# Memory attention and two MLPs on one core: PSUM tiles of two banks, table loads ahead of use, a root by Newton steps, and another order at the start

## The chip, the core and the metric

The kernel runs on one core of one Trainium2 chip. Five engines work side by side on that core, each with its own instruction queue: PE (TensorE, the matrix products), DVE (VectorE), ACT (ScalarE), POOL (GpSimd) and SP (SyncE, which here only starts transfers). Products land in PSUM, which has eight banks of 512 fp32 numbers for each of 128 partitions; everything else lies in SBUF. The metric is the device time of one execution in microseconds (us), the median of several runs.

## The reference, cut to what matters

There are 4 batches, 8 heads, 576 positions, a head width of 64 and 32 memory slots. The attention runs through the memory slots, and two MLPs follow on all 2304 positions of width 512.

```python
def _attn_ref(q, k, v, phi):
    a = np.exp(phi - np.max(phi, axis=2, keepdims=True))
    a = a / (np.sum(a, axis=2, keepdims=True) + 1e-09)      # over positions
    k_m = np.einsum('bhsm,bhsd->bhmd', a, k)
    v_m = np.einsum('bhsm,bhsd->bhmd', a, v)
    scores = 1.0 / np.sqrt(q.shape[-1]) * np.matmul(q, k_m.transpose(0, 1, 3, 2))
    scores = np.exp(scores - np.max(scores, axis=-1, keepdims=True))
    attn = scores / (np.sum(scores, axis=-1, keepdims=True) + 1e-09)   # over 32 slots
    return np.matmul(attn, v_m)

def _moe_ref(x, w_in, w_out):            # 512 -> 2048 -> 512
    h = x @ w_in
    return (h * (1.0 / (1.0 + np.exp(-1.702 * h)))) @ w_out

def _moe2_ref(x, w_gate, w_val, w_out, rms_g):   # 512 -> 1536 -> 512
    rms = np.sqrt(np.mean(x * x, axis=-1, keepdims=True) + 1e-06)
    xn = x / rms * rms_g
    g = xn @ w_gate
    return (g * (1.0 / (1.0 + np.exp(-g))) * (xn @ w_val)) @ w_out
```

## The kernel before

**Numbers in two parts.** Most products are made with operands split into a high part (fp32r) and a low part, the remainder: three products, high by high, low by high and high by low, stand for one of full precision. So each value that PE uses again is first copied by ACT (high part) and then subtracted by DVE or POOL (low part): `split()` at L858, `sub_lo()` at L744. Names that end in h and l, or an index 0 and 1, are such parts.

**Stages.** Batches are taken in pairs (pr 0 and 1), heads in two groups of four (g 0 and 1).

- Attention, for each batch and group: `att_k1t` or `att_k1` takes the maximum of phi over positions within a partition, `att_k2` and `att_k3` carry it over partitions (tiles pk2, pk3) and make the exponentials, `att_k4` multiplies them with k and v and makes their sums as products with a column of ones (tile pk4, `ones_f`), then the reciprocals rv, and `att_k5` brings km and vm into place (kz, vz, pk5). `att_q1` transposes q (pq1), `att_q3` makes the scores (pq3), their maximum and exponential, `att_q3s` the sums and the division, `att_q4` transposes the softmax result and splits it into attnT (pq4). Batch 0 is tiled by 64 positions: there the softmax result lies in two halves of the partitions, ACT copies it into a wider tile with zeros (`wide_e`, memset by DVE), and `att_q4` multiplies each of nine blocks with twin, a matrix of two stacked identities. Other batches are tiled by 96.
- First MLP, eight groups of 256 of the 2048 columns: `vm_part` multiplies the first weights into vm (tile pvm), so that `a_g1` (tile pg, lhsT vm, rhs attnT) gives the MLP's first layer at once; the first pg product from attnT and vm is what is called the first main product. The activation, a copy and a subtraction follow (gf, gr). `a_g2` multiplies gr with the second weights and DVE adds into x.
- Norm: `norm_1` squares and sums, `norm_2` sums over partitions by a product (pnr), ACT takes the root and DVE the reciprocal, `norm_3` and `norm_4` scale x.
- Second MLP, six groups of 256 columns as two units f each: `s_g3` makes gate and value by seven products of halves of the operands instead of eight, each product on 320 and 256 columns in a PSUM tile each (ps_A, ps_S), ACT copies out of PSUM, DVE adds and multiplies; `s_g4` multiplies with the output weights, 512 columns in a tile, and DVE adds into oacc; `put()` stores the rows.
- Weights come in blocks of 512 KB; ACT, DVE and POOL convert them (`w_conv`: pad, then a_inh and a_inl, or cv) and write them to caches in DRAM for the second pair.

**What sets the order.** All instructions of these steps go through one recorder and come from one line, L644, so tiles tell them apart. The steps are recorded in program order; class Plan groups them into units, gives each a due time (`dues()`: PE's main line is laid end to end, all else is due some time ahead of the unit that needs it), and simulates the five engines with a table of costs. `order()` takes at each step the unit that can start earliest, by due time among those that are near. Two tables change it: HASTE moves the due time of a named step earlier, OTHER moves single instructions of a named step between DVE and POOL. Where PE would idle ahead of a new PSUM tile, `fill()` puts dummy products of ones_r by ones_r (512 or 128 columns) into that tile. PSUM tiles are handed out in this order too:

```python
psp = pool("ps", 8, bass.MemoryType.PSUM, spare=2, ahead=4)
def psum(name):
    return psp.tile([P, 512], F32, tag="ps", name=name)
```

`can()` leaves spare slots for PE's main line, and ahead is how many tiles of the main line may be open before the due times press for the release of the oldest. An activation whose function lies in another table than the last one's makes the compiler put a table load right ahead of it on ACT.

## Time and profile before

| | before |
|---|---|
| median of 3 runs, us | 848.54 (847.63 to 848.97) |
| the profiled execution: its time, us | 843.96 |
| the profiled execution: its span, us | 842.2 |
| PE busy, us (share of the span) | 827.5 (98%) |
| DVE busy | 655.1 (78%) |
| ACT busy | 494.0 (59%) |
| POOL busy | 296.4 (35%) |

The span runs from the first to the last instruction of one profiled execution; the time of that execution lies 1.8 us above it. Busy time is summed over an engine's instructions, and PE's includes the dummy products and products that run at a lower clock. A row of the timeline holds consecutive instructions of one form with their start, their time together, and the idle time ahead of them with what ended it. An fp32 product (both operands fp32) shows as two records in a row of PE, a product of fp32r operands as one.

### The profile page before, as it was taken

What the parts mean: (1) busy time and instruction counts of PE and PEld (TensorE: products, weight loads), DVE (VectorE), ACT (ScalarE), POOL (GpSimd) and SP (SyncE); (2) the same over time, 40 slices, a digit from 0 to 9 for tenths busy, and PEclk for the clock granted to TensorE, in tenths of its full rate; (3) what the DMA queues carried; (4) which work ended last, traced back from release to release, by engine and by line L of the source; (5) the groups of instructions that cost most, each with busy time, mean ns of one, the idle gap of its engine ahead of it and who ended that gap; (6) DMA issues with size and microseconds to landing.
All of it is one profiled execution on the core that took longest, in us unless ns stands there. A gap on an engine that the chain in (4) does not pass through costs nothing.

```text
span 842.2 us, 16000 instructions
## 1 busy us (share of the span) xinstructions
PE 827.5 (98%) x5789; PEld 787.4 (93%) x5789; DVE 655.1 (78%) x1363; ACT 494.0 (59%) x1222; POOL 296.4 (35%) x295
## 2 busy tenths in 40 slices
PE   7999999999999999999999999999999999999997
PEld 6899999999999999999999999999999999999996
DVE  7978999999998998989989888767775435545555
ACT  4687878687778757666577755435552443323321
POOL 4444555666344556455846510120450000000000
PEclk9989999999999999999999999999999999999999
DMA  9964757856848776665676478463455543514314
GB/s 340 271 214 144 236 204 206 275 192 188 278 170 279 253 237 222 211 217 190 219 256 230 165 276 287 163 238 131 157 163 168 184 147 104 200 55 171 126 50 113
DMA packets 76767, 166.99 MB, mean 198 GB/s; under 512 B 7312, under 2 KB 29328, under 8 KB 76688
## 3 DMA queue, kind: packets, MB, share of 16 engines
q1 hardware_dynamic: 76688, 165.97, 59.5%
q8 instruction: 46, 0.75, 0.4%
q14 instruction: 33, 0.27, 0.1%
HBM read 106.69 MB, written 59.24 MB: 197 GB/s over the span
## 4 chain that ended last, share of the span: by engine, by line
PE 78%; DVE 10%; DMA 4%; issue 3%; ACT 3%; POOL 2%; SPq 0%; POOLq 0%; ACTq 0%; DVEq 0%
PE pg L644 42%; PE ps_A L644 21%; PE ps_S L644 9%; DVE pad L644 3%; PE pvm L644 2%; DVE x L644 2%; PE pq L644 2%; PE pk L644 1%; DMA stage<-in_q_dram 1%; DVE kmisc L644 1%; DVE stage L644 1%; DVE cv L644 1%; DMA stage<-in_v_dram 1%; DMA raw_c_gate<-in_moe_w_gate_dram 1%; DMA raw_a_out<-in_moe_w_out_dram 1%
## 5 line engine op out<-in xcount | busy, mean ns | idle before, releaser
L644 PE MATMUL pg<-gr,a_outh 128*128 128x384 f32 (+1 forms) x736 | 195.2, 334 | 0.8 <-POOL gr L644 0.6
L644 PEld LDWEIGHTS pg<-gr,a_outh 128*128 128x128 f32 x736 | 132.7, 188 | 2.4 <-POOL gr L644 2.0
L644 PE MATMUL pg<-gr,a_outl 128*128 128x384 f32 (+1 forms) x368 | 121.9, 331 | 0.0
L644 POOL TENSOR_TENSOR gr<-gf,gr 128x288 fp32r<-128x288 f32 (+2 forms) x118 | 83.8, 727 | 101.1 <-ACT gr L644 52.4
L644 PE MATMUL pg<-s_o,pp 128*128 128x512 f32 x432 | 114.0, 391 | 0.0
L644 ACT COPY c<-ps_A 128x320 f32<-128x320 f32 (+1 forms) x144 | 57.2, 399 | 93.7 <-PE ps_A L644 91.8
L644 DVE TENSOR_TENSOR x<-x,pg 128x384 f32<-128x384 f32 (+1 forms) x172 | 88.9, 535 | 11.0 <-PE pg L644 9.7
L644 DVE TENSOR_TENSOR oacc<-oacc,pg 128x512 f32<-128x512 f32 x90 | 61.7, 686 | 45.7 <-PE pg L644 44.9
L644 PEld LDWEIGHTS pg<-s_o,pp 128*128 128x128 f32 x432 | 79.0, 188 | 14.6
L644 PE MATMUL ps_A<-tba,s_A 128*128 128x320 f32 (+1 forms) x576 | 88.5, 296 | 0.0
L644 PEld LDWEIGHTS ps_A<-tba,s_A 128*128 128x128 f32 x576 | 81.9, 190 | 1.6
L644 DVE TENSOR_TENSOR c<-c,ps_S 128x320 f32<-128x320 f32 (+1 forms) x96 | 43.2, 452 | 37.6 <-PE ps_S L644 29.3
L644 PEld LDWEIGHTS pg<-gr,a_outl 128*128 128x128 f32 x368 | 69.1, 188 | 0.0
L644 ACT ACTIVATE gf<-pg 128x288 f32<-128x288 f32 x128 | 50.5, 412 | 31.1 <-PE pg L644 27.4
L644 ACT CAST gr<-gf 128x288 fp32r<-128x288 f32 (+2 forms) x184 | 59.2, 363 | 6.9 <-PE pg L644 4.3
L644 PE MATMUL pg<-s_o,tbd 128*128 128x512 f32 x216 | 61.1, 392 | 0.0
L644 DVE TENSOR_TENSOR c<-c 128x256 f32<-128x256 f32 (+1 forms) x86 | 39.3, 466 | 18.3 <-ACT c L644 16.6
L644 POOL TENSOR_SCALAR pad<-pad 128x512 f32<-128x512 f32 x20 | 41.2, 2062 | 19.9 <-ACT pad L644 19.7
L644 POOL TENSOR_SCALAR cv<-cv 128x512 f32<-128x512 f32 x20 | 44.1, 2210 | 8.1 <-ACT cv L644 6.5
L644 PE MATMUL ps_A<-tbc,s_S 128*128 128x256 f32 (+1 forms) x288 | 46.0, 297 | 0.0
L644 PE MATMUL ps_A<-tbd,s_A 128*128 128x320 f32 (+1 forms) x288 | 45.7, 297 | 0.1
L644 PE MATMUL ps_S<-tbb,s_S 128*128 128x256 f32 (+1 forms) x288 | 45.8, 296 | 0.0
(234 smaller groups left out, 1881.5 us busy)
## 6 DMA issues: line engine op xcount, KB each, us to landing
cache_s<-s_S SPq DMA_DIRECT2D x24, 512.0 KB, 3.7
s_S<-cache_s SPq DMA_DIRECT2D x24, 512.0 KB, 3.5
cache_b<-cv SPq DMA_DIRECT2D x36, 256.0 KB, 4.5
raw_a_in<-in_moe_w_in_dram SPq DMA_DIRECT2D x16, 512.0 KB, 5.3
raw_a_out<-in_moe_w_out_dram SPq DMA_DIRECT2D x16, 512.0 KB, 5.4
raw_c_gate<-in_moe_w_gate_dram SPq DMA_DIRECT2D x12, 512.0 KB, 4.7
raw_c_val<-in_moe_w_val_dram SPq DMA_DIRECT2D x12, 512.0 KB, 4.3
raw_c_o<-in_moe_w_out_dram SPq DMA_DIRECT2D x12, 512.0 KB, 4.4
```

The costliest lines, as they stand in the source:

```text
L644: getattr(self.real[op.eng], op.name)(*op.args, **op.kw)
```

## The change

- **PSUM.** Four tiles of two banks (`both()`) take the place of eight of one (`psum()` gives the first half of such a tile); spare goes from 2 to 1 and ahead from 4 to 2. Steps that used two tiles side by side now use one: `a_g1` both halves of its 256 columns, `a_g2` two blocks of 128 outputs, `s_g3` two times 288 columns instead of 320 and 256, `s_g4` two blocks of 128 positions, except in its last group. The instruction of ACT or DVE that empties a tile takes both banks at once (`pair()`), 576, 768 or 1024 columns. The SBUF pools follow: cv is 5 times 576 columns for 6 times 512, gp 3 tiles of double size for 6.
- **Order records.** A tile is tracked by bank (q, m), so a copy out of one bank doesn't order itself against writes of the other.
- **Table loads.** `issue()` puts a one-column activation (into the tile pre, from a constant) right ahead of each activation whose function lies in another table than the last one's. The load goes with it, and neither waits for the data of the activation behind them. The root leaves ACT, so its table is not loaded any more.
- **Norm.** `norm_2` makes the reciprocal root on DVE: a first value from the bits of x, then three Newton steps, on three columns.
- **Batch 0.** `att_k3s` adds up the nine blocks of exponentials to three column blocks (512, then 256 columns), and `att_k4` has three products with the column of ones for nine. `att_q4` transposes by 32-column pieces against the identity, 72 products for 18 with twin; the copies into the wide tile and twin are gone. The memset of the stage tile goes from DVE to ACT.
- **Other batches.** `att_k1` (a strided reduction) is replaced by `att_k1t` (additions of the maximum kind), the sum in `att_k3s` likewise. `att_q1`, `att_q3`, `att_q3s` and `att_q4` treat both halves in one instruction.
- **Planner.** HASTE and OTHER are new, and some costs are changed. The tail of the last group is recorded as nine single tiles.

Counts by the recorded order: DVE 1365 instructions before and 1026 after, ACT 1224 and 776, POOL 297 and 217. The columns and number of PE's main products stay.

```diff
-SETS = {AF.Exp: 1, AF.Gelu_apprx_sigmoid: 2, AF.Silu: 3, AF.Sqrt: 4}
+SETS = {AF.Exp: 1, AF.Gelu_apprx_sigmoid: 2, AF.Silu: 3}
...
-        "a_g1 0 0 1": 19.4,
...
+        "w_load a 0 0 out 1": 615.4,
...
-                    q, m, write = 15, 1, True
+                    c = x.offset % 1024
+                    far = c + sum(st * (n - 1) for st, n in list(x.ap)[1:])
+                    q, m, write = 15, (1 if c < 512 else 0) | (2 if far >= 512 else 0), True
...
+            table = None
             for _, _, op in self.order():
+                func = op.kw.get("func") if op.eng == "ACT" else None
+                if func in SETS and SETS[func] != table:
+                    table = SETS[func]
+                    self.real["ACT"].activation(out=self.pre, in_=self.one, func=func)
                 getattr(self.real[op.eng], op.name)(*op.args, **op.kw)
...
-    cvp = pool("cv", 6, spare=3)
+    cvp = pool("cv", 5, spare=2)
...
-    gpp = pool("gp", 6)
+    gpp = pool("gp", 3)
...
-    psp = pool("ps", 8, bass.MemoryType.PSUM, spare=2, ahead=4)
+    psp = pool("ps", 4, bass.MemoryType.PSUM, spare=1, ahead=2)
...
+    def both(name):
+        return psp.tile([P, 1024], F32, tag="ps", name=name)
+
     def psum(name):
-        return psp.tile([P, 512], F32, tag="ps", name=name)
+        return both(name)[:, :512]
+    def pair(x, n):
+        return x.rearrange("p (q n) -> p q n", q=2)[:, :, :n]
...
     def att_k3s(u, eng):
         km = kmisc[u]
+        if u[0] < N9:
+            y = kmisc[u, "sums"] = cv("y")[:, :512]
+            e = stage[u][:, 3456:4480]
+            eng.tensor_tensor(out=y, in0=e[:, :512], in1=e[:, 512:], op=ALU.add)
+            eng.tensor_tensor(out=y[:, :256], in0=y[:, :256], in1=y[:, 256:], op=ALU.add)
+            return
...
     def att_q4(u, par):
-            for i, c in enumerate(some(par)):
-                PE.matmul(
-                    ps[:, R9 * i : R9 * i + R9], lhsT=qm[:, 3456 + P * c : 3456 + P * c + P], rhs=twin,
-                    start=True, stop=True,
-                )
+            for i in range(len(some(par))):
+                for o in range(4):
+                    t, rows = o // 2, slice(R9 * (o % 2), R9 * (o % 2) + R9)
+                    PE.matmul(
+                        ps[32 * o : 32 * o + 32, R9 * i : R9 * i + R9], lhsT=sm[rows, i, t],
+                        rhs=ident[rows, rows], start=True, stop=True,
+                    )
...
     def norm_2(pr, t):
-        A.activation(
-            out=r[:, 0, 0:3], in_=ps[:, 0:TB:P], func=AF.Sqrt, bias=epst, scale=1.0 / DM
+        V.tensor_scalar(
+            out=x, in0=ps[:, 0:TB:P], scalar1=1.0 / DM, scalar2=EPS, op0=ALU.mult, op1=ALU.add
         )
-        V.reciprocal(out=r[:, 1, 0:3], in_=r[:, 0, 0:3])
+        V.tensor_scalar(
+            out=zi, in0=x.bitcast(U32), scalar1=1, scalar2=None, op0=ALU.logical_shift_right
+        )
+        V.tensor_scalar(
+            out=yi, in0=zi, scalar1=-1.0, scalar2=float(0x5F3759DF), op0=ALU.mult, op1=ALU.add
+        )
+        for i in range(3):
+            V.tensor_tensor(out=z, in0=y, in1=y, op=ALU.mult)
+            V.scalar_tensor_tensor(out=z, in0=z, scalar=-0.5, in1=x, op0=ALU.mult, op1=ALU.mult)
+            V.scalar_tensor_tensor(out=y, in0=z, scalar=1.5, in1=y, op0=ALU.add, op1=ALU.mult)
...
-            for q in range(2):
-                product(pr, q, "S3", "T3", f, part[q]["a"])
-                x = part[q]["v"]
-                A.copy(out=x, in_=part[q]["a"])
-                V.tensor_tensor(out=x, in0=x, in1=part[q]["b"], op=ALU.add)
-                A.activation(out=x, in_=x, func=AF.Silu)
+            product(pr, "S3", "T3", f, part["a"])
+            x = full(part["v"])
+            A.copy(out=x, in_=pair(part["a"], HALF))
+            V.tensor_tensor(out=x, in0=x, in1=pair(part["b"], HALF), op=ALU.add)
+            A.activation(out=x, in_=x, func=AF.Silu)
...
-    for step in late + waiting:
-        line(*step)
-    plan.ones = ones_r
+    for kk in range(PT // P):
+        line(s_g4, 1, NB - 1, kk, False)
+    plan.ones, plan.one, plan.pre = ones_r, ones_f, pre
```

**Three places in the order.** The first is SP's queue from the program's start: kmisc is phi, stage holds k, v and q of a batch and group, raw_a are blocks of the first MLP's weights. Before:

```order
L644 DMA kmisc0_0_114<-in_phi_dram 128x288 x2
L644 DMA raw_a_0_0_in_0_118<-in_moe_w_in_dram 128x2x512
L644 DMA raw_a_0_0_in_1_119<-in_moe_w_in_dram 128x2x512
L644 DMA stage0_0_115<-in_v_dram 128x2x576
L644 DMA stage0_0_115<-in_k_dram 128x2x576
L644 DMA kmisc0_1_116<-in_phi_dram 128x288
L644 DMA raw_a_0_0_out_0_156<-in_moe_w_out_dram 128x1024
L644 DMA kmisc0_1_116<-in_phi_dram 128x288
L644 DMA stage0_0_115<-in_q_dram 128x2x576
```

After:

```order
L593 DMA raw_a_0_0_in_0_117<-in_moe_w_in_dram 128x2x512
L593 DMA raw_a_0_0_in_1_118<-in_moe_w_in_dram 128x2x512
L593 DMA raw_a_0_0_out_0_155<-in_moe_w_out_dram 128x1024
L593 DMA kmisc0_0_113<-in_phi_dram 128x288 x2
L593 DMA kmisc0_1_115<-in_phi_dram 128x288 x2
L593 DMA stage0_0_114<-in_k_dram 128x2x576
L593 DMA stage0_0_114<-in_v_dram 128x2x576
L593 DMA stage0_1_116<-in_k_dram 128x2x576
L593 DMA stage0_1_116<-in_v_dram 128x2x576
```

Three weight blocks now stand ahead of phi, and k and v of both groups come ahead of both q.

The second is DVE's queue at the same place, behind the constants: pad is a weight block under conversion, y and kmisc carry the maximum of phi. Before:

```order
L1602 TENSOR_TENSOR twin_93<-ident_90 128x64
L644 MEMSET stage0_1_117 128x1152
L644 TENSOR_TENSOR y_123<-kmisc0_0_114 128x192
L644 TENSOR_TENSOR y_123<-y_123,kmisc0_0_114 128x192
L644 TENSOR_TENSOR kmisc0_0_114<-y_123 128x64
L644 TENSOR_TENSOR kmisc0_0_114<-kmisc0_0_114,y_123 128x64
L644 TENSOR_REDUCE kmisc0_0_114<-pk2_124 64x2
L644 TENSOR_TENSOR kmisc0_0_114<-kmisc0_0_114,pk3_125 128x576
L644 TENSOR_SCALAR pad_120<-pad_120 128x512 x3
```

After:

```order
L593 TENSOR_SCALAR pad_119<-pad_119 128x512 x2
L593 SCALAR_TENSOR_TENSOR pad_119<-raw_a_0_0_in_0_117,pad_119 128x512
L593 TENSOR_SCALAR pad_119<-pad_119 128x512
L593 SCALAR_TENSOR_TENSOR pad_119<-raw_a_0_0_in_0_117,pad_119 128x512
L593 TENSOR_SCALAR pad_119<-pad_119 128x512
L593 SCALAR_TENSOR_TENSOR pad_119<-raw_a_0_0_in_1_118,pad_119 128x512
L593 TENSOR_TENSOR y_122<-kmisc0_0_113 128x192
L593 SCALAR_TENSOR_TENSOR pad_119<-raw_a_0_0_in_1_118,pad_119 128x512
L593 TENSOR_TENSOR y_122<-y_122,kmisc0_0_113 128x192
L593 TENSOR_TENSOR y_140<-kmisc0_1_115 128x192
L593 TENSOR_TENSOR kmisc0_0_113<-y_122 128x64
```

The memset and twin are gone, weight steps have moved ahead of the first maximum, and the second group's maximum stands among the first group's.

The third is PE in the second MLP of the second pair, near the end: ps_A11, ps_A12 and ps_S1 are tiles of `s_g3`, pg4 of `s_g4`. Before:

```order
L644 MATMUL ps_A11_1681<-tba1_1419,s1_11_A11_1662 128x320 x6
L644 MATMUL pg4_1674<-s1_8_o2_1600,pp_1626 128x512 x3
L644 MATMUL pg4_1674<-s1_9_o2_1622,tbd1_1422 128x512 x3
L644 MATMUL ps_A11_1682<-tba1_1419,s1_11_A11_1662 128x256 x6
L644 MATMUL ps_A12_1683<-tba1_1419,s1_11_A11_1662 128x320 x6
L644 MATMUL ps_A11_1681<-tbb1_1420,s1_11_S1_1663 128x320 x6
L644 MATMUL ps_A11_1682<-tbb1_1420,s1_11_S1_1663 128x256 x6
L644 MATMUL ps_A12_1684<-tba1_1419,s1_11_A11_1662 128x256 x6
L644 MATMUL ps_S1_1687<-tbb1_1420,s1_11_S1_1663 128x320 x6
L644 MATMUL ps_S1_1688<-tbb1_1420,s1_11_S1_1663 128x256 x6
L644 MATMUL ps_A11_1681<-tbc1_1421,s1_11_S3_1664 128x320 x6
L644 MATMUL ps_A11_1682<-tbc1_1421,s1_11_S3_1664 128x256 x6
```

After:

```order
L593 MATMUL ps_A11_1191<-tbb1_1019,s1_11_S1_1179 128x288 x12
L593 MATMUL ps_A12_1192<-tba1_1018,s1_11_A11_1178 128x288 x12
L593 MATMUL ps_A11_1191<-tbc1_1020,s1_11_S3_1180 128x288 x12
L593 MATMUL pg4_1195<-s1_8_o2_1138,pp_1155 128x512 x3
L593 MATMUL pg4_1195<-s1_9_o2_1153,tbd1_1021 128x512 x3
L593 MATMUL pg4_1195<-s1_8_o2_1138,pp_1155 128x512 x3
L593 MATMUL pg4_1195<-s1_9_o2_1153,tbd1_1021 128x512 x3
L593 MATMUL ps_A11_1191<-tbd1_1021,s1_10_A22_1165 128x288 x12
L593 MATMUL ps_S1_1194<-tbb1_1019,s1_11_S1_1179 128x288 x12
```

The products of 320 and 256 columns into two tiles have become 12 of 288 into one, and three products or more still stand between the first product on a tile and the next that is added onto it (ps_A11 and ps_A12 here).

## Rows read from the trace of the kernel before

**Rows 1.** The page, part 1: busy time, share of span, instructions.

```profile
PE 827.5 (98%) x5789; PEld 787.4 (93%) x5789; DVE 655.1 (78%) x1363; ACT 494.0 (59%) x1222; POOL 296.4 (35%) x295
```

**Rows 2.** The chain of waits, its end: start us, us, what.

```profile
823.47 1.60 PE ps_S L644 x12
825.07 12.28 PE pg L644 x54
```

**Rows 3.** Table by windows: stretch, us, busy us (count) by engine, PEclk, DMA, GB/s.

```profile
0.00:20.00 20.00, 15.46 (x130) 12.66 (x131) 15.27 (x40) 9.41 (x19) 9.26 (x14) 1.00 0.94 336
...
40.00:60.00 20.00, 19.03 (x177) 18.41 (x178) 15.24 (x39) 15.34 (x44) 9.84 (x11) 0.83 0.67 212
...
180.00:200.00 20.00, 19.86 (x137) 18.90 (x137) 19.93 (x43) 17.11 (x45) 16.49 (x16) 1.00 0.72 245
```

**Rows 4.** Timeline of PE: start us, us, op, out<-in, shapes, xcount [idle before, releaser].

```profile
1.25 3.62 PE L644 MATMUL pk<-ones_r 128*128 128x512 f32 x10 [1.25 <-DVE ones_r L1604]
...
10.36 2.19 PE L644 MATMUL pk<-stage 128*64 128x128 f32 x36 [1.83 <-DMA stage<-in_k_dram]
12.48 2.17 PE L644 MATMUL pk<-ones_f,stage 128*128 128x1 f32 x18
...
25.41 1.55 PE L644 MATMUL pq<-twin,stage 128*128 128x64 f32 x12
...
36.42 1.52 PE L644 MATMUL pk<-stage,kmisc 96*32 96x128 f32 x48
...
38.12 0.94 PE L644 MATMUL pq<-ident,stage 96*128 96x96 f32 x9
...
45.12 2.13 PE L644 MATMUL pq<-kmT,stage 128*96 128x64 f32 x12
...
47.01 0.83 PE L644 MATMUL pg<-attnT,vm_0h 128*128 128x288 f32 x2
...
50.98 1.15 PE L644 MATMUL pq<-kmT,stage 128*96 128x64 f32 x12
```

**Rows 5.** Timeline of DVE, 0 to 60 us.

```profile
3.98 0.30 DVE L644 TENSOR_TENSOR y<-kmisc 128x192 f32<-128x192 f32 x1
...
12.35 1.41 DVE L644 TENSOR_TENSOR y<-kmisc 128x192 f32<-128x192 f32 x1 [0.21 <-DMA kmisc<-in_phi_dram]
...
15.02 0.15 DVE L644 TENSOR_SCALAR rv<-pk 128x1 f32<-128x1 f32 x1
```

**Rows 6.** Timeline of ACT, 0 to 60 us.

```profile
7.92 1.36 ACT L644 ACTIVATE stage<-kmisc 64x576 f32<-64x576 f32 x2
```

**Rows 7.** Timeline of POOL, 0 to 60 us.

```profile
12.27 2.61 POOL L644 TENSOR_TENSOR a_inl<-pad,a_inh 128x512 fp32r<-128x512 f32 x2 [3.33 <-ACT a_inh L644]
14.85 2.02 POOL L644 TENSOR_SCALAR pad<-pad 128x512 f32<-128x512 f32 x1
...
40.70 1.46 POOL L644 TENSOR_SCALAR rv<-maskeo,rv 128x3 f32<-128x3 f32 x1 [1.09 <-DVE rv L644]
```

**Rows 8.** Groups by form: names, shapes, xcount | busy us, mean ns | idle before, releasers.

```profile
L644 DVE TENSOR_TENSOR x<-x,pg 128x384 f32<-128x384 f32 x156 | 81.8, 544 | 9.6 <-PE pg L644 8.4
...
L644 DVE TENSOR_TENSOR oacc<-oacc,pg 128x512 f32<-128x512 f32 x90 | 61.7, 686 | 45.7 <-PE pg L644 44.9
...
L644 ACT ACT_TABLE_LOAD x28 | 35.9, 1283 | 2.7 <-PE pg L644 1.5 <-PEq L1807 0.7
...
L644 ACT COPY c<-ps_A 128x320 f32<-128x320 f32 x72 | 30.7, 426 | 52.5 <-PE ps_A L644 51.7
```

**Rows 9.** Tile x, 100:240: DVE's additions (ns min/median/max); below, idle before (us, times).

```profile
L644 DVE TENSOR_TENSOR x<-x,pg x65: 441/542/555, 100.5 to 239.2; 128x384 f32<-128x384 f32 x62, 128x288 f32<-128x288 f32 x3
...
  PE pg L644: 1.6, 2
```

**Rows 10.** Waits of PE, 60 to 240 us: total us, times, longest.

```profile
PE pvm L644 <- DVE a_inl L644: 0.8, 1, 0.8
...
PE pg L644 <- POOL gr L644: 0.2, 1, 0.2
```

More of the change, by code (lines that the diff above doesn't have):

```diff
@@ L1238, in att_q3s @@
         eng.tensor_tensor(out=sm, in0=sm, in1=over_m(y), op=ALU.mult)
-        if u[0] < N9:
-            c = some(hp)
-            for r in range(2):
-                rows = slice(R9 * r, R9 * r + R9)
-                A.copy(out=wide_e(u)[rows, c[0] : c[-1] + 1, :, r], in_=sm[rows])
     def att_q4(u, par):
@@ new lines, in places @@
+    def places(pr, f):
+        if f % 3 == 0:
+            x = tb[pr, "tbd"][:, 1].rearrange("p y e n -> p y (e n)")
+            return [(0, x)]
+        if f % 3 == 1:
+            x, y = [gpp.tile([P, 2, 2, TB], F32R, tag="gp", name="pp") for i in range(2)]
+            part["rest"] = y[:, 1]
+            return [(0, x.rearrange("p a y n -> p (a y n)").rearrange("p (y n) -> p y n", y=2)), (2 * TB, y[:, 0])]
+        x = gpp.tile([P, 2, 2, TB], F32R, tag="gp", name="pp")
+        return [(0, part["rest"]), (TB, x.rearrange("p a y n -> p (a y n)").rearrange("p (y n) -> p y n", y=2))]
@@ L1521, in s_g3, with full @@
     def s_g3(pr, f, k):
+        def full(x):
+            return x.rearrange("p (q n) -> p q n", q=2)
         if k == 0:
-            c = [cvp.tile([P, 512], F32, tag="cv", name="c")[:, :320] for i in range(4)]
-            part[0] = dict(zip(("p", "u", "v", "s"), c))
-            c = [vlp.tile([P, 512], F32, tag="vl" + x, name="c") for x in "hl"]
-            part[1] = dict(zip(("p", "u", "v", "s"), [x[:, o : o + 256] for x in c for o in (0, 256)]))
-            for q in range(2):
-                part[q]["a"] = product(pr, q, "A11", "B11", f)
-                A.copy(out=part[q]["p"], in_=part[q]["a"])
@@ L1601 @@
     make_identity(nc, ident)
-    nc.vector.tensor_tensor(out=twin, in0=ident[:, :R9], in1=ident[:, R9:], op=ALU.add)
     nc.vector.memset(ones_f, 1.0)
@@ L1778 @@
                 late += waiting
-                waiting[:] = [(s_g4, int(key[0] == "s"), f // 2, kk) for kk in range(9)]
+                waiting[:] = [(s_g4, int(key[0] == "s"), f // 2, kk) for kk in range(5)]
         elif width(*key[1:]) == HALF:
```

531 lines of the change are left out of this document (293 added, 238 removed), and 119 rows, old and new, of the table OTHER.

## Prediction

> **What bounds the kernel now.** The page comes first: PE is busy 98% of the span, the next engine, DVE, 78% [rows 1]. Busy is not full rate, so I then looked at PE's steps in the chain of waits. Near the end twelve products (320 or 256 columns) take 1.60 us, and the last 54, of 512 columns, take 12.28 us, 0.227 us each, back to back [rows 2]. The change leaves the number and the columns of the main products as they are (six of 320 and six of 256 columns become twelve of 288, the same 3456). So the main work has a fixed price, and only time in which PE lacks work can be won. The table by windows shows where that is [rows 3]: PE is busy 15.5 us of the first 20, and 19.9 from 180 to 200 us, where DVE has no room left (19.9 of 20). [...] The same 12 records of a product take 2.13 us at 45.12 and 1.15 us at 50.98 [rows 4].
>
> The start is worse than its idle time says, because the planner puts dummy products into gaps (from ones_r, into the next tile). They count as busy: ten records and 3.62 us at 1.25 [rows 4], 33 wide ones by the order ahead of the first main product, which starts at 47.01 us (pg from attnT). I followed the chain that leads there: k and v of batch 0 land (PE waits to 10.36), products with k, their sums against a column of ones, the softmax on DVE and POOL, the transposition by twin, the splitting into two parts [rows 4 to 7].
>
> **The change part by part.** *Sums by fewer products.* Per head group, nine products with a one-column operand become three. Nine take 2.17 us at 12.48 (18 records, two a product) [rows 4], 0.24 each; 12 fewer: -2.9 us of PE work, all ahead of the first main product. In their place stand two additions per group, over 512 and 256 columns: about 0.69 and 0.40 us on DVE by the rows by form [rows 8], 1.3 us for 512 on POOL [rows 7], where the order puts one of each width. *Transposition.* 18 products with twin (six, twelve records, take 1.55 us, 0.26 each [rows 4]) become 72 with 32-column weights. Nearest is the row of 24 products with such weights and twice the columns (1.52 us for 48 records, 0.063 a product [rows 4]): that is the upper end, 4.6 us against 4.7, half of it the lower. I take 0.05, 3.6 us: -1.1 us. Eight ACT copies of the softmax result leave the same chain. These savings count inside the start below, not beside it.
>
> *The order of the start.* Three weight blocks now load ahead of phi, k and v, and eight DVE steps on weights stand ahead of the first group's first maximum. I walked the new order with durations from before. At 336 GB/s [rows 3] the three blocks of 512 KB take some 5 us, k and v of the first group are in at 12 us, of the second at 15, both q at 19. DVE's weight steps, at 0.4 to 0.7 us by their 512 columns [rows 8], put the last maximum near 11 us; until then 30 dummy products of 0.23 to 0.36 us fill PE. Both groups now go side by side: exponentials end at 15 and 17 us (9.3 for the first group before [rows 6]), both k products with their sums at 22 us, one group's reciprocals wait behind a POOL step of 1.46 us [rows 7], the scores are there at 24 and 28 us, the softmax steps of both groups (some 20 DVE steps of 0.2 to 0.55 us, with one POOL step on weights of 2.0 us among POOL's multiplications [rows 7]) end at 36, and the first main product starts at **37 us**, the value I take. The ends: 33 if no POOL step stands in the way; 42 by the first rival.
>
> From 47.0 to 37.0 is -10.0 us, but not all of it is won. Work of batch 1 that stood ahead of 47.0 now follows: 24 products with their sum 1.7 us, twelve transpositions of q 1.3, scores 1.1 [rows 4], six products with wide 0.8 (half of twelve [rows 2]), small ones an estimated 0.6: +5.5. Net **-4.5 us** (-8.5 to +0.5). Right after 37 us PE needs wide, which ACT and DVE split only behind attnT, and then vm of the second group, four more splits with some 3 us of other DVE steps ahead; the order has four dummy products there. I put PE's waits to 60 us at **+1.5 us** net (0 to +3). [...]
>
> *Wider steps on the other engines.* DVE's addition from PSUM takes 544 ns over 384 columns and 686 over 512 [rows 8]: 1.1 ns a column and 0.12 us fixed. The order has 1026 DVE instructions for 1365, although the Newton steps add 69 at 0.15 us or a little more (the step on one column takes 0.15 [rows 5]), 10 to 14 us. Some 400 removed at 0.12 us are 48 us; with the memsets and the strided sums gone too, DVE falls by about 40 of 655 us, by about 12 of 135 from 100 to 240 us. PE's named waits from 60 to 240 us are five, of 0.8 to 0.2 us [rows 10], 1.8 us together, and I estimate as much again in late starts inside rows that count as busy. Their cause, a full DVE queue and what waits for it, is mostly removed: **-3.5 us** (0 to -5). ACT and POOL do the same columns in half the instructions and are not full [rows 1]. Seven table loads of 1283 ns leave ACT, 21 one-column activations come. Their cover is ACT's idle time (41%); without it 9 us would count. The load stood right ahead of the instruction that needs it, and ACT's idle time before all 28 that PE ended is 1.5 us [rows 8]: loading early is worth that at most, and I count it at nothing.
>
> *Two-bank tiles.* Where a product is added onto a tile that was just copied, the order has other products between, at all 96 such places: at least six of 512 columns, 1.36 us, against a copy of 576 columns of at most 0.77 us (426 ns for 320, in proportion [rows 8]). Past the start a slot is nearly always written again 1.6 us or more after its last product (before: 2.7 or more, by the same steps). **+0.5 us** (0 to +17, third rival). The end stays: single tiles, then an addition and the store.
>
> **Sum.** -4.5 + 1.5 - 3.5 + 0.5 = **-6.0 us**: span 842.2 to 836.2. The profiled execution took 843.96 us, 4.6 less than the median of the runs, 848.54; I carry the difference over: **842.5 us**, by itself 837 to 846.5.
>
> **Rivals.** *The start is no earlier.* DVE's addition over 192 columns takes 0.30 us at 3.98 and 1.41 us at 12.35 [rows 5], while POOL runs two subtractions of SBUF operands (12.27 to 14.88) [rows 7]. The change puts two additions, a subtraction and a weight step on POOL between 15 and 21 us, beside DVE's additions and subtractions of the same chain. If four of these are held up by 1.1 us each, the first main product starts at 41 to 42: net +0.5, +2 after it, -2.5 in the middle: 848.5 us. For it: these two rows. Against: few of DVE's steps at 15 to 21 us are on the chain itself. [...] *Everything goes as ordered.* Start at 33, no new waits, all waits of the middle gone: -8.5 - 5 = -13.5: 835 us. Against it: before, the order held 33 wide dummy products, at most 12 us at 0.36, while PE lacked work for some 21 of the first 47 us. *Slower: half as many PSUM slots.* From 100 to 240 us DVE waited for PE ahead of only 2 of 65 additions into x [rows 9]: it is late, and sets when a slot is free. With four slots PE has half the lead. If DVE stays full, each of the 86 double additions holds PE for the smallest named wait of before, 0.2 us: +17 us, and the 3.5 are not won: 863 us, 854 if half of them wait. It decides by DVE's busy time in those windows; I expect 18 of 20, it needs over 19.3.
>
> **How the numbers follow.** Forecast 0.57, as ordered 0.16, start no earlier 0.12, slower 0.15. About 0.2% (1.7 us) is what a measurement here can tell from no change, so 846.8 to 850.2 is "same". Faster: 0.57 + 0.16, less a little at the edge, 0.72; same 0.13; slower 0.15. The range leaves out the third rival and what of the second lies below 832: 832 to 850.
>
> **What would show it.** Right: the first pg product from attnT at 35 to 39 us, the one-column products at 0.7 us per group; DVE near 615 us busy and 18 of 20 from 100 to 240. Wrong: a first main product after 41 us; PE waiting for DVE x or ACT c after 60 us; steps of twelve products over 1.60 us; the 72 products over 0.06 us each.

## The result

The changed kernel takes **839.38 us** (median of four runs, 839.12 to 841.09), the kernel before 848.75 us beside it: a ratio of 0.9894, 95% interval 0.9875 to 0.9912. That is 9.4 us less where 6.0 were forecast, and inside the range of 832 to 850. The profiled execution took 841.09 us, its span 839.3. Its span is thus only 2.9 us below the 842.2 from which the sum started; the sum put it at 836.2.

The page of the changed kernel, part 1, and its table by windows (columns as in [rows 1, 3]):

```profile
PE 823.3 (98%) x5890; PEld 784.5 (93%) x5890; DVE 620.0 (74%) x1024; ACT 435.8 (52%) x774; POOL 259.6 (31%) x215
```

```profile
0.00:20.00 20.00, 16.95 (x111) 14.29 (x112) 13.97 (x38) 10.67 (x15) 9.16 (x14) 1.00 0.94 332
...
40.00:60.00 20.00, 19.90 (x225) 18.44 (x224) 15.52 (x35) 17.83 (x40) 14.82 (x12) 1.00 1.02 260
...
120.00:140.00 20.00, 17.28 (x140) 16.32 (x138) 15.41 (x29) 15.42 (x30) 5.87 (x6) 0.83 0.53 175
...
180.00:200.00 20.00, 20.00 (x183) 19.54 (x182) 19.04 (x33) 14.29 (x29) 9.32 (x10) 1.00 0.52 177
```

Three things are to be seen. DVE fell from 655.1 to 620.0 us, and from 19.93 to 19.04 of 20 us at 180. The fall of the clock at 40 us [rows 3], in that trace to 0.50 from 42 to 48 us, is gone. And a new one has come, at 120 to 140 us: a mean granted clock of 0.83 (0.50 from 132 to 136 us) where it was 1.00 before, with PE busy for only 17.28 of 20 us.

The timeline of PE at the start (columns as in [rows 4]):

```profile
18.28 0.61 PE L593 MATMUL pk<-ones_f,y 128*128 128x1 f32 x4
18.75 0.36 PE L593 MATMUL pk<-ones_f,stage 128*128 128x1 f32 x2
...
32.26 0.88 PE L593 MATMUL pq<-ident,stage 64*32 64x64 f32 x48 [0.56 <-POOL stage L593]
...
36.52 0.53 PE L593 MATMUL pg<-attnT,vm_0h 128*128 128x288 f32 x2
```

The three one-column products of a group take 0.8 us by their rows (18.28 to 19.11) where nine took 2.17; 24 of the new transposition products take 0.88 us, 0.037 each; the first main product stands at 36.5 us, where it stood at 47.01 [rows 4].

Groups by form (columns as in [rows 8]), and the tile x from 100 to 240 us (as in [rows 9]):

```profile
L593 DVE TENSOR_TENSOR x<-x,pg 128x768 f32<-128x768 f32 x78 | 73.7, 947 | 17.6 <-PE pg L593 16.9
L593 ACT COPY c<-ps_A 128x576 f32<-128x576 f32 x72 | 46.0, 639 | 96.6 <-PE ps_A L593 94.5 <-DVE r L593 0.9 <-issue 0.7
...
L592 ACT ACT_TABLE_LOAD x20 | 25.7, 1283 | 0.3
```

```profile
L593 DVE TENSOR_TENSOR x<-x,pg x32: 933/946/955, 104.4 to 232.9; 128x768 f32<-128x768 f32 x32
...
  PE pg L593: 8.4, 7
```

An addition of two tiles at once takes 947 ns where two single ones took 544 each. DVE now waits for PE ahead of 7 of 32 additions, 8.4 us in all; before it was 2 of 65 and 1.6 us [rows 9]. DVE is no longer late by rule, and the windows of 20 us from 100 to 240 us hold 17.6 us of its work in the mean, so the third rival, which needed over 19.3, is out. What PE waits for from 60 to 240 us (columns as in [rows 10]):

```profile
PE pk L593 <- ACT gf L593: 2.7, 1, 2.7
PE pvm L593 <- ACT vlh L593: 1.6, 1, 1.6
PE pg L593 <- POOL gr L593: 0.4, 1, 0.4
PE pg L593 <- DVE vm_0l L593: 0.3, 1, 0.3
PE pq L593 <- POOL stage L593: 0.3, 1, 0.3
```

DVE's a_inl of [rows 10] is gone from the list. ACT now leads it, with one wait of 2.7 us: that is the place at 120 to 140 us.

### The profile page after: what moved, and what is told of

It reads as the page before. It is cut to its first block, busy times and chain, and to the rows that moved or that the text cites. A ratio compares the mean times of both kernels' runs of the same rounds, so it can differ in the third digit from the quotient of the medians.

```text
span 839.3 us, 15263 instructions
## 1 busy us (share of the span) xinstructions
PE 823.3 (98%) x5890; PEld 784.5 (93%) x5890; DVE 620.0 (74%) x1024; ACT 435.8 (52%) x774; POOL 259.6 (31%) x215
## 4 chain that ended last, share of the span: by engine, by line
PE 87%; DVE 5%; ACT 3%; DMA 2%; issue 2%; POOL 1%; SPq 0%; POOLq 0%; DVEq 0%; ACTq 0%
PE pg L593 49%; PE ps_A L593 22%; PE ps_S L593 9%; PE pk L593 3%; PE pvm L593 2%; PE pq L593 2%; DVE pad L593 1%; DVE stage L593 1%; DMA raw_c_o<-in_moe_w_out_dram 1%; ACT L592 1%; DVE x L593 1%; DMA raw_b_vg<-cache_b 1%; DVE cv L593 0%; DMA raw_a_in<-in_moe_w_in_dram 0%; DVE vm_0l L593 0%
## 5 line engine op out<-in xcount | busy, mean ns | idle before, releaser
L593 ACT COPY c<-ps_A 128x576 f32<-128x576 f32 x72 | 46.0, 639 | 96.6 <-PE ps_A L593 94.5
L593 DVE TENSOR_TENSOR x<-x,pg 128x768 f32<-128x768 f32 (+1 forms) x86 | 79.7, 929 | 20.7 <-PE pg L593 20.0
L593 DVE TENSOR_TENSOR oacc<-oacc,pg 128x1024 f32<-128x1024 f32 (+1 forms) x54 | 56.1, 1041 | 51.3 <-PE pg L593 50.8
L593 PE MATMUL ps_A<-tba,s_A 128*128 128x288 f32 x576 | 83.5, 295 | 0.0
L593 POOL TENSOR_TENSOR gr<-gf,gr 128x576 fp32r<-128x576 f32 (+2 forms) x53 | 58.6, 1117 | 62.2 <-ACT gr L593 51.9
L593 ACT ACTIVATE gf<-pg 128x576 f32<-128x576 f32 x64 | 41.2, 647 | 35.0 <-PE pg L593 33.5
L593 ACT CAST gr<-gf 128x576 fp32r<-128x576 f32 (+2 forms) x92 | 45.6, 527 | 7.1 <-PE pg L593 5.8
L593 PEld LDWEIGHTS pg<-s_o,tbd 128*128 128x128 f32 x216 | 39.6, 188 | 7.2
L593 PE MATMUL ps_A<-tbb,s_S 128*128 128x288 f32 x288 | 42.3, 295 | 0.1
L593 PE MATMUL ps_S<-tbb,s_S 128*128 128x288 f32 x288 | 42.2, 295 | 0.0
```

What stands on the lines that cost most here:

```text
L593: getattr(self.real[op.eng], op.name)(*op.args, **op.kw)
```

## The experiments

### Once more, both kernels

> The changed kernel once more, nothing edited. In its first trace PE waited 2.72 us at 127 us for a PSUM slot that a late gelu held, and the granted clock fell behind it; that stretch (120 to 145 us) lost 7.5 us, while the other timed executions were 1.6 to 2 us shorter than the one with the trace. Theory A, the order itself holds the wait (two table loads, three copies of vm and two weight steps of ACT stand ahead of that gelu): the wait at the start of the pk product near 127 us is there again with 2 us or more, and 120 to 140 us again has a mean clock near 0.83. Theory B, it is chance of one execution (steps of DVE and POOL that met): no wait over 0.5 us there, clock 1.00, span 835 or less. Time 839 to 841 by A, 834 to 837 for the traced execution by B.

It takes 839.63 us (838.66 to 841.64). The wait is there again, to a tenth of a microsecond, and so is the clock. Waits of PE, and the window:

```profile
PE pk L593 <- ACT gf L593: 2.7, 1, 2.7
```

```profile
120.00:140.00 20.00, 17.30 (x140) 16.33 (x138) 15.43 (x29) 15.60 (x31) 6.06 (x6) 0.83 0.52 174
```

Theory A: the wait stands in the order. The 1.6 us for ACT vlh at 237 us is not there a second time; that one is chance.

> The kernel before once more. Its traced execution took 843.96 us, its timed ones 845.6 to 850.4. Theory A, what differs between its executions are waits at a few places, each with a fall of the clock: a trace of 846 or more shows at least one window of 20 us with a mean clock under 0.9 besides 40 to 60 us, or a named wait over 1 us that the first trace hasn't. Rival B, everything is a little longer: products step 0.3% slower throughout, no new window.

It takes 846.19 us (844.67 to 848.13), the traced execution 846.03. Its window from 40 to 60 us:

```profile
40.00:60.00 20.00, 19.05 (x161) 18.38 (x162) 13.93 (x37) 14.14 (x39) 9.56 (x10) 0.74 0.57 189
```

Its mean granted clock is 0.74, for the 0.83 of [rows 3]: the stretch at the lower clock is longer. Both traces hold the same instructions of PE in the same order. Taken one by one, those of the second trace fall behind by 1.4 us from 45 to 60 us and by 0.5 us more at 130 to 135 us; the rest is smaller and goes both ways. So most of what differs lies at a fall of the clock, as theory A has it, but in the old window: the sign that theory A named, a new window or a new wait over 1 us, is not there. Also to be noted: the 843.96 us of the first trace is below every timed run of this kernel in five comparisons (lowest 844.13). My 4.6 us between trace and median are no constant of the kernel.

### Why ACT is late at 127 us

The timeline of ACT, then parts of those of DVE and POOL, in the first trace of the changed kernel:

```profile
116.79 0.68 ACT L593 CAST gr<-gf 128x576 fp32r<-128x576 f32 x1
119.56 0.62 ACT L593 CAST a_outh<-pad 128x512 fp32r<-128x512 f32 x1 [2.10 <-DVE pad L593]
120.09 0.64 ACT L593 ACTIVATE gf<-pg 128x576 f32<-128x576 f32 x1
...
122.12 1.28 ACT L592 ACT_TABLE_LOAD   x1
...
124.26 2.07 ACT L593 CAST vm_4h<-pvm 64x1024 fp32r<-64x1024 f32 x3
126.35 0.67 ACT L593 ACTIVATE pad<-raw_a_in 128x512 f32<-128x512 f32 x1
126.93 0.60 ACT L593 CAST a_outh<-pad 128x512 fp32r<-128x512 f32 x1
127.55 1.28 ACT L592 ACT_TABLE_LOAD   x1
...
129.07 0.65 ACT L593 ACTIVATE gf<-pg 128x576 f32<-128x576 f32 x1
```

```profile
115.16 2.33 DVE L593 TENSOR_TENSOR a_inl<-pad,a_inh 128x512 fp32r<-128x512 f32 x1
...
118.28 1.25 DVE L593 SCALAR_TENSOR_TENSOR pad<-raw_a_out,pad 128x512 uint32<-128x512 uint32 x1
```

```profile
114.82 2.12 POOL L593 TENSOR_TENSOR kmisc<-kmisc 96x768 f32<-96x768 f32 x1 [2.42 <-ACT kmisc L593]
117.55 1.44 POOL L593 TENSOR_TENSOR gr<-gf,gr 128x576 fp32r<-128x576 f32 x1 [0.61 <-ACT gr L593]
```

Read from the end: PE's pk product needs the PSUM slot of pg, which the gelu at 129.07 frees. Ahead of that gelu stand two table loads, three copies, two weight steps, and at 117.5 us a cast that waited 2.10 us for DVE with a ready gelu behind it. DVE was late by two of its steps, each beside work of POOL: its subtraction at 115.16 took 2.33 us while POOL's subtraction ran from 114.82 to 116.94, and the weight step at 118.28, which that cast needs, took 1.25 us while POOL's next one ran from 117.55 to 118.99. The same two forms take 0.69 us (at 120.22) and 0.68 us (at 122.77) elsewhere on DVE. In this trace the two forms (the subtractions for a_inl and a_outl, and pad from raw_a, all of 512 columns) take at most 0.69 us wherever POOL is idle beside them, and 0.67 to 2.33 us where it works; what decides between these is not shown. That is the coincidence of [rows 5, 7] once more, not at the start, where the first rival had put it, but here.

The edit gives the places in the listing (its planned times, in us) at which single rows stand instead, and the rest keeps its order:

```diff
...
+            at = {
+                ("w_conv a 0 4 out 0", "copy"): 118.60,
+                ("w_conv a 0 5 in 1", "activation"): 127.20,
+                ("w_conv a 0 4 out 1", "copy"): 127.21,
+                ("w_conv a 0 5 in 1", "POOL"): 128.90,
+                ("w_conv a 0 4 out 1", "POOL"): 127.44,
+                ("w_conv a 0 4 out 1", "dma_start"): 127.30,
+            }
...
```

> The changed kernel with three steps of weight conversion moved at one place, all other rows in their order: on ACT the cast into a_outh that stood blocked behind DVE's pad steps (2.10 us idle at 117.5 us) comes behind the next gelu and its two copies, and the next pad step and cast come behind the gelu that frees the PSUM slot; the pad step that POOL then made goes to DVE, and POOL makes the gr subtraction ahead of the a_outl one. Both traces of the changed kernel have PE waiting 2.7 us there for that gelu, and the clock at the lower level behind it. Theory A, this one late gelu costs some 6 us: the wait falls to 1.4 us or less, 120 to 140 us has a mean clock of 1.00, the time falls by 4 to 6.5 us, to 833 to 836. Rival B, DVE is behind anyway and the next tile waits instead: time within 1.5 us of the changed kernel.

It takes 836.34 us (836.00 to 837.47). This run carried one more step of POOL to 127 us, behind its reader, so that a part of one group's output weights was converted from the wrong values; the amount of work is the same. So the gain could still have come from that step's absence at 110 us. The next run leaves it in its place, since it moves only rows that the listing has after 116 us.

> As the run fix1, but with the other pad step of POOL, at 110 us, left in its place (fix1 carried it behind its reader, so that its output was not the kernel's). In fix1 the wait at 127 us fell from 2.7 to under 0.9 us, the clock stayed up, and waits of 1.2 us for ACT kz at 133 and 1.0 us for ACT gf at 147 us were left. Theory A, the late gelu alone: the wait again under 1.4 us, mean clock 1.00 from 120 to 140, time 835 to 837. Rival B, the gain of fix1 came from POOL's step that was out of the way at 110 us: the wait 2 us or more, the time within 1.5 us of the changed kernel's 839.5.

It takes **835.40 us** (835.26 to 836.48), ratio to the kernel before 0.9863 (0.9820 to 0.9906). The timeline of ACT and of PE, and the window:

```profile
124.89 1.28 ACT L609 ACT_TABLE_LOAD   x1
...
126.41 0.65 ACT L610 ACTIVATE gf<-pg 128x576 f32<-128x576 f32 x1
```

```profile
127.11 1.52 PE L610 MATMUL pk<-stage,kmisc 96*32 96x128 f32 x48 [0.37 <-ACT gf L610]
```

```profile
120.00:140.00 20.00, 19.55 (x179) 18.30 (x178) 19.34 (x37) 14.71 (x28) 7.08 (x7) 1.00 0.62 204
```

Theory A. The gelu comes 2.7 us earlier, the wait is 0.37 us, the clock stays up, and the time is 4.1 us below the mean of 839.5 of the two medians of the changed kernel. To place it I compare with the second trace of the changed kernel, because the first also holds the chance wait of 1.6 us at 237 us. Instruction by instruction of PE, this run is 2.6 us ahead at 130 us, where the wait has gone, and 4.9 us at 140, where the unedited trace has been through the lower clock; 0.9 us then go to a new wait for a gelu at 145 us, and at the end it is 4.3 us ahead. So 2.3 us are the wait (2.70 to 0.37), and most of the rest goes with the lower clock behind it. The two steps of DVE still take 2.33 and 1.25 us here: the run shows what ACT's blocked queue cost, not what the meeting of DVE and POOL does. This version is faster than both kernels. Three rows of ACT have moved, one row of POOL has gone to DVE, two of POOL have changed places, and one transfer has moved with them.

### One part back at a time, in the kernel's own order

Three runs change the program where it is issued, so that every other row stays in its place. Their medians are compared with 839.5 us. They were not all timed beside the unedited kernel, and the median of the kernel before lies between 846.70 and 848.75 us in the five comparisons, so each difference is open by 1 or 2 us.

The early loads are left out:

```diff
...
-                if func in SETS and SETS[func] != table:
-                    table = SETS[func]
-                    self.real["ACT"].activation(out=self.pre, in_=self.one, func=func)
```

> The changed kernel without the one-column activations ahead of the table loads; all other instructions stand in the same order. My prediction counted the early loads at nothing, at most the 1.5 us of idle time ahead of ACT's loads. Theory A: within 1.5 us of the changed kernel, with ACT's own waits ahead of the gelu and exponential groups up by the same. Rival B: four PSUM tiles make PE depend on ACT's punctuality, each of some 20 loads of 1.28 us that now begins after the data comes shows as a wait of PE: slower by 5 to 15 us.

It takes 840.83 us (840.26 to 841.04), 1.2 us above the unedited kernel beside it, whose own executions reach from 838.66 to 841.64 and so cover all of these. ACT's idle time ahead of its loads is 2.3 us, where it was 0.3. Theory A holds; that the early loads are worth anything is not shown.

The wide steps are made as two:

```diff
...
+                if op.eng != "PE" and op.step.split(" ")[0] in ("a_g1", "a_g2", "s_g3", "s_g4"):
+                    if len(shape) == 3 and shape[1] == 2:
+                        parts = 2
+                for i in range(parts):
...
+                        kw = {k: x[:, i : i + 1] if hasattr(x, "tensor") else x for k, x in kw.items()}
```

> The changed kernel in its own order and with its PSUM tiles, but every instruction of ACT, DVE and POOL in a_g1, a_g2, s_g3 and s_g4 that takes two banks or two blocks at once is made as two, one behind the other: 233 more on DVE, 298 more on ACT, 53 more on POOL. It takes back the wider steps alone. Theory A, the term DVE relief of my sum (-3.5 us, 0 to -5): the time rises by 2 to 6 us, DVE has some 28 us more (0.12 us each) and stands over 19 of 20 us from 100 to 240 us, PE's waits for gf, gr and x come up there. Rival B, the relief is worth nothing because the waits left are those for slots and late ACT steps: within 1 us. Third, four slots make it worse than the kernel before was: 10 us or more.

It takes 843.41 us (842.20 to 845.71), **3.9 us more**. The group of x, the sum of its windows from 100 to 240 us, and PE's waits from 240 to 480 us, where the unedited trace has none named in its first profile and one of 0.5 us in its second:

```profile
L602 DVE TENSOR_TENSOR x<-x,pg 128x384 f32<-128x384 f32 x156 | 78.7, 547 | 13.6 <-PE pg L602 13.3
```

```profile
sum 140.00, PE 136.44 PEld 132.97 DVE 125.70 ACT 100.79 POOL 75.80; mean PE 19.49 PEld 19.00 DVE 17.96 ACT 14.40 POOL 10.83
```

```profile
PE pg L602 <- DVE gr L602: 1.4, 3, 0.8
PE pg L602 <- DVE attnT L602: 0.4, 1, 0.4
PE pg L602 <- DVE x L602: 0.2, 1, 0.2
```

Theory A holds by the time, and by the place it misses. DVE rose by 10 to 14 us in all, not 28. From 100 to 240 us it is busy for 125.7 us, between the 122.9 and 127.6 of the two unedited traces, and PE stands no further back at 240 us than in those. Of the 2.4 us by which this trace, that of the shortest of ten executions, is longer than the second unedited one, 2.0 come from 360 to 455 us, the most at 383 us with a wait of 0.8 us for gr.

The root goes back to ACT, where the first Newton step stood:

```diff
+                if step.startswith("norm_2") and nth > 5:
+                    if nth == 6:
...
+                        self.real["ACT"].activation(
+                            out=op.kw["out"], in_=op.kw["in0"], func=AF.Sqrt, bias=self.epst, scale=1.0 / 512
+                        )
+                    elif nth == 17:
+                        self.real["DVE"].reciprocal(out=op.kw["out"], in_=self.seen["root", step])
+                    continue
```

> The changed kernel in its own order, with the root back on ACT where the first Newton step stood (a one-column activation ahead of it where the table changes) and the reciprocal on DVE where the last one stood; the other Newton steps are left out. The run root, listed anew, lost 9.7 us, of which 4.2 us are one wait of PE for vm at 347 us behind such a load, and some from another order. Theory A, with the order kept the root costs little: within 2 us of the changed kernel. Rival B, a table load in the middle of ACT's queue holds the slots: slower by 3 to 7 us, with a named wait of PE for ACT or for vm between 230 and 480 us.

It takes 844.60 us (841.91 to 847.00), **5.1 us more**. PE's waits from 240 to 480 us, then ACT at one of the places:

```profile
PE pnr L606 <- DVE r L600: 1.2, 1, 1.2
...
PE pg L606 <- ACT gr L606: 0.5, 1, 0.5
PE pg L606 <- POOL gr L606: 0.5, 1, 0.5
PE pg L606 <- ACT r L596: 0.4, 1, 0.4
```

```profile
456.10 1.28 ACT L593 ACT_TABLE_LOAD   x1
457.40 0.20 ACT L593 ACTIVATE pre<-ones_f 128x1 f32<-128x1 f32 x1
457.51 0.24 ACT L596 ACTIVATE r<-pnm,epst 128x3 f32<-128x3 f32 x1
...
459.67 1.28 ACT L605 ACT_TABLE_LOAD   x1
```

Rival B. The six roots cost ACT ten loads more (30 for 20), one in and one out unless two roots follow each other, and behind them stand copies that PE needs: PE waits for r and for gr. Instruction by instruction of PE this trace equals the second unedited one to 0.2 us from 37 to 280 us and is 3.7 us behind at the end. It loses 2.2 of them at three places (284, 299 and 329 us, waits for POOL gr, ACT gr and ACT r) and 1.4 at the pnr product at 462 us. Those 1.4 are not all the root's: its reciprocal stood where the last Newton step had, and DVE came to it late. So the root costs 2.2 to 3.7 us by this trace, and 5.1 by the median.

### Edits that were listed anew

In these runs the planner makes a new order from the edited steps, so that the order of all engines changes along with the edit.

> The changed kernel with batch 0's sums (nine one-column products per group, no additions ahead) and transposition (nine products with twin, ACT copies into the wide tile) as before; the planner lists the order anew. Theory A, the smaller products make the start earlier: the first main product comes 5 to 7 us later than 36.5 us (2.7 us of one-column products, 3.0 of twin products, eight copies on ACT), and the time rises by 4 to 7 us. Rival B, the order of loads and weight steps makes it (three weight blocks first, both groups side by side): the first main product within 2.5 us of 36.5, the time up by 2 us or less.

It takes 858.51 us (857.84 to 859.12). The start (twin and nine sums back, code as in the kernel before):

```profile
18.09 2.17 PE L593 MATMUL pk<-ones_f,stage 128*128 128x1 f32 x18
...
35.17 2.65 PE L593 MATMUL pq<-twin,stage 128*128 128x64 f32 x12 [0.73 <-ACT stage L593]
...
38.17 5.38 PE L593 MATMUL pq<-twin,stage 128*128 128x64 f32 x24
43.31 0.83 PE L593 MATMUL pg<-attnT,vm_0h 128*128 128x288 f32 x2
```

The first main product comes 6.8 us later, as theory A has it, but about half of that goes with the lower clock, which came here (mean 0.80 from 20 to 40 us, 0.86 from 40 to 60): 36 records of twin take 8.03 us, where twelve at 25.41 had taken 1.55 [rows 4], which is 3.4 us more. The other 3.4 are less than the 5 to 7 that theory A gives to the smaller products. The rest of the 19 us comes later in the program, where the edit is long over and only the listing differs.

> The changed kernel with s_g4 in single tiles of 512 columns and their single additions everywhere, as its last group has them; s_g3 keeps two banks. In the first trace a step of 512 columns in the second MLP takes 228.0 ns in the mean, before 230.3, and the stretch from 480 us to the end is 2.6 us shorter than before, without a named wait in either. Theory A, half as many hand-overs of tiles between PE and the emptying engines shorten the steps: the mean step of 512 columns goes back to 229.5 to 230.5 ns, the time rises by 0.7 to 1.5 us; DVE's busy time grows by some 6 us and costs nothing. Rival B, the steps are shorter for another reason: they stay at 228, the time within 0.5 us.

```diff
-                late = waiting[: 1 + f % 2]
+                late = waiting[: 2 if f % 2 == 0 else 3]
...
-                waiting[:] = [(s_g4, int(key[0] == "s"), f // 2, kk) for kk in range(5)]
+                waiting[:] = [(s_g4, int(key[0] == "s"), f // 2, kk, False) for kk in range(9)]
```

It takes 852.53 us (850.60 to 852.64). The steps of 512 columns stay at 227.8 ns: rival B on that question. The loss lies elsewhere: some 9 us in the trace, all between 360 and 470 us, in waits and dummy products of the new listing.

> The changed kernel with the root on ACT and the reciprocal on DVE as before (loads of that table come back, with a one-column activation ahead of each; the eleven Newton steps per tile on DVE go); the planner lists it anew. My prediction put the Newton steps at 10 to 14 us of DVE, hidden, and the loads at nothing. Theory A: within 2.5 us of the changed kernel, DVE's busy time 8 to 14 us less, ACT's 4 to 9 us more. Rival B, the loads matter now that slots are few: slower by 4 us or more, with waits of PE for ACT between 230 and 480 us, where the norm lies.

It takes 849.23 us (847.22 to 851.27), 9.7 us more; up to 5.1 of it are the root's by the run that keeps the order.

> The changed kernel with three PSUM tiles of two banks for four (the planner lists it anew). Theory A, four are near the limit, as the slower rival of the prediction has it: PE's named waits for ACT gf, DVE x and ACT c sum to over 15 us from 60 us on, the time rises by 15 us or more. Rival B, four leave room: the time rises by less than 6 us.

```diff
-    psp = pool("ps", 4, bass.MemoryType.PSUM, spare=1, ahead=2)
+    psp = pool("ps", 3, bass.MemoryType.PSUM, spare=1, ahead=2)
```

It takes 871.09 us (two executions, 869.14 and 873.03). PE's waits from 60 us on sum to 19.1 us by name (5.3 with four tiles); the first of them:

```profile
PE pg L593 <- ACT gf L593: 2.7, 2, 1.6
PE pg L593 <- DVE x L593: 2.1, 4, 1.1
PE ps_A L593 <- ACT c L593: 2.0, 2, 1.2
```

These three are waits for slots, and the time is theory A's. The waits that theory A named (ACT gf, DVE x, ACT c) come to 9.1 us only, not to over 15, and the rest of the 19.1 is also for data. This listing is new too, so the 31.6 us are no price of a slot.

> The changed kernel with HASTE and OTHER empty; the planner lists it by its own rules. The three edits that were listed anew (oldstart, narrow, root) rose by 19.0, 13.0 and 9.7 us, more than the edits explain: narrow keeps the changed kernel's landmarks to 360 us and then loses 6 to 8 us up to 460 us. Theory A, the tables are fitted to the exact list of steps, and any edit that shifts it gives up a part of their worth: without them the time rises by 12 us or more, over the 848 of the kernel before. Rival B, the tables matter little and those three edits cost what they cost: the time rises by less than 5 us.

It takes 868.40 us (867.10 to 869.33): without HASTE and OTHER the changed kernel would be 20 us slower than the kernel before. The tables are worth 29 us, and three edits that shift the list of steps gave up 5 to 13 us of that. So an edit that is listed anew tells little of its own cost; only landmarks ahead of the first difference, and the runs in the kernel's own order, do.

## Where the prediction was right, and where not

The time fell inside the range, and the start held. The rest of the sum came out by luck: its terms missed in both directions, one was right in size and wrong in place, and three that were put at nothing or almost nothing were not. The four runs that undo one thing each are compared with 839.5 us.

| step of the prediction | put at, us | measured, us | by |
|---|---|---|---|
| start, and waits right after it | -4.5 + 1.5 = -3.0 | -3.2 (estimate) | PE's work done by 60 us, two traces |
| wider steps of DVE, ACT, POOL | -3.5 (0 to -5) | -3.9, at another place | halves |
| root off ACT, Newton steps on DVE | 0 | -5.1 (-2.2 to -3.7 by the trace) | root_same |
| early table loads | 0 (1.5 at most) | -1.2, not clear of noise | nopre |
| two-bank tiles | +0.5 (0 to +17) | +4.1 at one place | fix2 |
| main products | 0 | -2.4 | from the 850,000th column to the end, two traces |
| sum | -6.0 | -11.7; the kernel: -7.5 and -9.4 | |

The measured terms do not add up to the whole, and need not: each was taken with the others in place, and a wait that goes lets another take its place. Two comparisons gave 7.5 and 9.4 us for the whole. None of these runs takes back the new order as such, the new HASTE and OTHER, so what the changed order is worth by itself stays open.

**The start** was right, to half a microsecond at the first main product (37 forecast, 36.5). For the net I estimate every step of PE at what its form takes at a granted clock of 1.00 in these traces, dummies left out: by 60 us PE had done 28.1 us of such work before and 25.8 after, and 5.5 us less of it are to be done in all (sums and transposition); 28.1 - 25.8 - 5.5 gives -3.2. PE's main products agree: their 50,000th column comes at 71.9 us for 75.3, their 100,000th at 96.6 for 100.2. So the time without such work (dummies, waits and slow clock together) did not shrink, it went from 31.9 to 34.2 us; the gain is the work that went away. One size inside was off: the 72 transposition products take 0.037 us or less by the row, not 0.05, inside the bounds of 0.032 and 0.063. A fall of the clock at 30 to 37 us is chance: of the six traces with this very order there, it is missing in both of the changed kernel and in fix2, and there in halves, root_same and fix1 (mean granted clock 0.91 from 20 to 40 us), after the same waits of 0.6 and 0.7 us. It costs 0.0 to 0.4 us at the next products of PE, which would else wait for POOL.

**The wider steps** were right in size and in DVE's sum (620.0 us, 615 forecast), but not in their place. From 100 to 240 us DVE has 122.9 us for 135.3 in the first traces, the 12 us less that were forecast, and 127.6 for 133.9 in the second ones, 6.3 less. The term was to come from PE's waits between 60 and 240 us. The run halves gives DVE no more work there and loses its time after 360 us. So the size is in part luck, and how the wide steps save time is not shown beyond the waits for gr there.

**The root** is the step that failed most. I costed the Newton steps by DVE's length, rightly, and then looked for what the loads cost only in ACT's idle time ahead of them [rows 8]. That is what a load delays in itself. What it delays behind it, copies that free slots and the chain from the root to the pnr product, I left to ACT's idle share of 41%. A mean over the span does not say that the idle time lies where the load is. In place of nothing the root on ACT measured 5.1 us by the medians.

**The two-bank tiles.** The mechanism was named as the third rival: a late engine holds a slot, and four slots give half the lead. It came true at one place, with ACT as the late engine and not DVE, and there it cost 4.1 us. My check was a count of columns between writes of a slot, "1.6 us or more after its last product"; it left out that the emptying step itself can stand behind a blocked row. No run gives this order eight tiles, so how much of the 4.1 us is due to the tiles and how much to the order of ACT's queue stays open.

**The main products** were taken as fixed. From the 850,000th column of main products (those of vm not counted) to the end the kernel before took 336.9 us and the changed one 334.5, in both traces of the latter; 0.3 of the 2.4 us come behind the last product. Two steps of 288 columns take 265.0 ns, of 320 and 256 together 266.2; a step of 512 takes 227.8 for 229.9. The first is some 1.1 us over 1000 pairs, the second 1 us. The cause of the second stays open: the tile's width was ruled out by the run narrow, and nothing else was tried.

**Trace and median.** I carried 4.6 us from the trace of before over to the forecast. The traces of the changed kernel lie 1.7 us above and 0.2 us above their medians, so nothing is to be carried over. Without it the sum would have said 838, a little below what was measured; with it 842.5. By the spans alone the two traces of the changed kernel are 2.9 and 4.2 us below the first trace of the kernel before, and 4.9 and 6.2 below its second (844.2), so the spans show less than the medians do, in part because the first trace was a short one. The first rival (848.5) is out by the start. The second (835) is out by its start at 33 us, where 36.5 was measured, and by the wait at 127 us; that the run fix2 comes to its time, 835.4, doesn't bear it out, for it came there another way.

## What to carry to other kernels

The wide tiles saved instructions on the engines that empty them (by the run halves 233 on DVE, 298 on ACT and 53 on POOL) and left the engine that fills them four slots for eight; look for each place where the emptying step stands behind a row that may block, for one such place cost as much (4.1 us) as all wide steps gained (3.9). A switch of activation tables is to be priced by what queues behind it, not by idle time ahead of it: the ten loads more of root_same went with 2.2 to 5.1 us, while all 28 of the kernel before had 2.7 us of idle time ahead of them [rows 8]. And where a listing is fitted by tables, an edit is measured by holding the order, or it measures the listing.

## What was not expected of the hardware

- A switch of tables took 1.28 us and no more here: all 20 loads in the first trace of the changed kernel take 1283 ns, with 0.3 us of idle time ahead of them in all, and at the place shown for root_same the load begins at 456.10, 0.01 us after the copy ahead of it has ended, and ends at 457.38, and the next activation begins at 457.40.
- The wait at 127 us was followed by the lower clock in all seven traces that have it (2.4 to 3.2 us long; mean granted clock from 120 to 140 us 0.83 in both of the changed kernel, 0.91 in halves); where it was 0.37 us, or a wait was 0.9 us at 145 us or 1.6 us at 237 us, the clock stayed at 1.00. Yet at 32 us the lower clock (mean 0.91 from 20 to 40 us) came in three of six traces with the same order and the same waits of 0.6 and 0.7 us.
- The two traces of the changed kernel agree to 0.1 us at every instruction of PE from 10 to 130 us, five engines and all transfers notwithstanding; those of the kernel before part at 47 us, where its clock has fallen (0.83 and 0.74 in the mean from 40 to 60 us).
- 24 products of 32 columns of weights and 64 of data, written to four groups of 32 partitions from two halves of 64 rows, take 0.88 us: 0.037 us each.
